# A decode step of sliding-window attention plus an MLP on one core: the order of V, w2 and P V, where 1/sum is applied, and which engine makes the tables

## The chip, the cores and the metric

The kernel runs on one core of a Trainium2 chip. The metric is device time in microseconds (us) of one execution. TensorE (PE) multiplies matrices, VectorE (DVE) and ScalarE (ACT) work elementwise, GpSimd (POOL) does here only memsets and small tables, and SyncE (SP) issues the transfers. Each engine runs its own program in order, and semaphores order the engines among each other. The transfers issued by SyncE go through one queue, over 16 DMA engines, in the order of issue.

## The reference

One token, x of 1024 elements, goes through a layer norm; the result feeds an attention with a cache and an MLP, and both are added to x's sum:

```python
def _A_ref(x, k_cache, v_cache, wq, wo):      # x: [1, 1, 1024]
    W = 4096                                  # the last 4096 of 65536 positions
    q = (x @ wq).reshape(1, 1, 32, 128).transpose(0, 2, 1, 3)
    k = jnp.repeat(k_cache[:, :, Sk - W:, :], 8, axis=1)     # 4 kv heads for 32 heads
    v = jnp.repeat(v_cache[:, :, Sk - W:, :], 8, axis=1)
    p = _softmax(jnp.einsum("bhqd,bhkd->bhqk", q, k) * 128 ** -0.5)
    o = jnp.einsum("bhqk,bhkd->bhqd", p, v)
    return o.transpose(0, 2, 1, 3).reshape(1, 1, 4096) @ wo

def _B_ref(x, w1, b1, w2, b2):
    h = _gelu(_layernorm(x) @ w1 + b1)        # 1024 -> 3584
    return h @ w2 + b2                        # 3584 -> 1024

xn = _layernorm(x)
return x + _A_ref(xn, ...) + _B_ref(xn, ...)
```

All inputs are bf16. Read are w1 and w2 (7.3 MB each), the windows of K and V (4.2 MB each), wq and wo (8.4 MB each): nearly 40 MB for one token.

## The kernel before

With one row of activations, every weight is read once and streams through TensorE as the moving operand, 512 columns at a time; the stationary operand is a column of 128 activations, padded to 32 columns. Matmuls of that shape use a quarter of the array, so several go side by side into different groups of 32 partitions.

**Transfers.** SyncE issues W1, K (two halves) and wq (two halves) at once. Then it waits for the product with W1 (`C["h"]`, L365) and issues w2, which takes W1's place in SBUF, and V in two halves (`load_cache`, L366 and L367). V's region is not free from the start: the row of b1 is laid in it (`B1R`, L138), and matmuls read it ahead of the product with W1. After the product with wq (`C["q"]`, L480), SyncE issues wo in six pieces of 16, 8, 4, 2, 1 and 1 rows of blocks (`WO_CHUNKS`), into wq's place.

**The order on TensorE.** Everything is written out by hand, and loops are rolled: `rolled` (L161) makes a loop whose body holds the matmuls of one step, with addresses in registers; a semaphore may be waited for in each round, against the register `trip`. In order: the norm's sums; b1 (L350); h = y W1 in 8 rounds (L362); transposes of h; q in 8 rounds, as the halves of wq come; transposes of q and its copies into `LB`; the scores, 32 matmuls (L470), with one maximum for each half; the maximum turned and spread (L492, L501) into `BIAS`. Then `steps("w2", ...)` (L506), 4 rounds of 14 matmuls into the accumulator `acc` (bank 7 of PSUM). ScalarE meanwhile takes the exponential in four quarters (L508), and VectorE transposes each quarter into `PT` (L512). TensorE then makes the sums of the rows with a matmul against `SAME` (L518), and runs P V (L529), 4 rounds of 8 matmuls, into bank 4.

**From P V to O.** VectorE takes the reciprocal of the sums (L533) and multiplies the masks `BLK` with it into `RG` (L535), four scalars for each partition. P V leaves four blocks of 128 columns, of which each partition needs one: ScalarE copies the first scaled by `RG[:, 0]` (L540), VectorE adds the three others scaled likewise (L543), into `OD`. Four matmuls against `E4` (L551) put `OD` in the layout that wo needs, and a copy (L555) writes it into `VEC` as `OT`.

**wo and the end.** `steps("wo", ...)` (L560) runs 3 rounds of 8 rows as the first two pieces land, four rows follow one by one, and the last four rows are cut into four quarters of 256 columns, which go side by side into another bank (L569). While these last rows come, ScalarE and VectorE copy the accumulated rows out into `PART` (L585); one add (L590) joins both, and a transfer of 2 KB writes the result.

**Tables.** VectorE makes, between the norm and the first transposes of K, the zeros of `LB`, `VEC` and `E4` and the tables `BLK`, `HD`, `REP4`, `SAME` and `E4` from an identity that GpSimd has filled (L296 to L315).

Of the kernel before, what the change touches and what calls it, by code (L numbers as in the profile page):

```python
# [10 lines left out]
D = 1024  # L11
# [40 lines left out]
def bass_parallel_sum__sliding_block_cached__mixer_channel_mlp__decode_kernel(  # L52
# [43 lines left out]
    E4 = sb("E4", [128, 4 * 129], f32)  # L96
    HD = sb("HD", [128, 2 * HQ], f32)
    REP4 = sb("REP4", [128, 4 * 128], bf16)
# [19 lines left out]
    U2 = sb("U2", [128, FC], f32)  # L118
    VEC = sb("VEC", [128, FC + 32 + PAD], bf16)
    GT = VEC[:, 0:FC]  # L120
    OT = VEC[:, FC:FC + 32]
    MXP = sb("MXP", [128, 3], f32)
# [5 lines left out]
    REC = sb("REC", [128, 1], f32)  # L128
    RG = sb("RG", [128, 4], f32)
    OD = sb("OD", [128, DH], f32)  # L130
# [29 lines left out]

    def rolled(label, n, streams, body, sem=None, ready=None):  # L161
        places = []
        for (view, step, weights), regs in zip(streams, (wregs, vregs)):
            span = bass.RuntimeValue.of_register_unchecked(zero, min_val=0, max_val=step * (n - 1))
            aps = view(span)
            low = pe.lower_ap(aps[0], for_matmul_weights=weights)
            pe.reg_add(regs[0], bass_rust.RegisterHandle(low.regref, pe.engine), 0)
            places.append([(mybir.RegisterAccessPattern(
                ap=low.ap, dtype=low.dtype, memsetref=low.memsetref, regref=reg.name,
                is_regloc_offset=low.is_regloc_offset, reg_ap_offset=reg.name, const_ap_offset=low.const_ap_offset,  # L170
                const_sub_tensor_id=low.const_sub_tensor_id, bass_ap=ap),
                reg, 2 * (ap.offset.min_val - aps[0].offset.min_val)) for ap, reg in zip(aps, regs)])
        pe.reg_mov(trip, 1)
        if ready is not None:
            pe.wait_ge(DVE.sem, ready)
        pe.br(f"L_{label}")
        nc.switch_bb(f"L_{label}", parent=None)
        if sem is not None:
            pe.wait_ge(sem, trip)
        for place in places:  # L180
            for _, reg, by in place[1:]:
                pe.reg_add(reg, place[0][1], by)
        last = body([p for p, _, _ in places[0]], [p for p, _, _ in places[1]])
        for place, (_, step, _) in zip(places, streams):
            pe.reg_add(place[0][1], place[0][1], 2 * step)
        pe.reg_add(trip, trip, 1)
        pe.br_lt(trip, n + 1, on_true=f"L_{label}", on_false=f"E_{label}")
        nc.switch_bb(f"E_{label}", parent=None)
        return last
# [41 lines left out]
    POOL.mark(pool.memset(OUTM[:, :], OUTSIDE))  # L231
    C["mask"] = fill(OUTM[:, :].rearrange("k (s g) -> k s g", g=2), [[0, 256], [1, 2]], 0, -1, value=0.0)


# [20 lines left out]
    for r in range(KC):  # L255
# [39 lines left out]
    C["zo"] = DVE.mark(dve.memset(PS[:, 4 * 512:5 * 512], 0.0))  # L295
    C["lb"] = DVE.mark(dve.memset(LB[:, :], 0.0))  # L296
    DVE.mark(dve.memset(VEC[:, :], 0.0))
    DVE.mark(dve.memset(E4[:, :], 0.0))
    dve.wait_ge(POOL.sem, C["identf"])
    DVE.mark(dve.tensor_reduce(out=BLK[:, :], in_=identf[:, :].rearrange("p (i q h) -> p q i h", i=NPAIR, q=4),  # L300
                               axis=AX.XY, op=ALU.add))
    DVE.mark(dve.tensor_reduce(out=HD[:, 0:HQ], in_=identf[:, :].rearrange("p (q h) -> p h q", q=4),
                               axis=AX.X, op=ALU.add))
    DVE.mark(dve.tensor_reduce(out=HD[:, HQ:2 * HQ].rearrange("p (i h) -> p i h", i=NPAIR),
                               in_=identf[:, :].rearrange("p (i q h) -> p i h q", i=NPAIR, q=4), axis=AX.X, op=ALU.add))
    C["rep4"] = DVE.mark(dve.tensor_copy(
        REP4[:, :].rearrange("p (e q d) -> p e q d", e=4, q=4),
        identf[:, :].rearrange("p (e d) -> p e d", e=4).unsqueeze(2).to_broadcast([128, 4, 4, 32])))
    dve.wait_ge(DVE.sem, DVE.cnt)
    C["same"] = DVE.mark(dve.tensor_copy(  # L310
        SAME[:, :].rearrange("p (i q h) -> p i q h", i=NPAIR, q=4),
        HD[:, 0:HQ].rearrange("p (i h) -> p i h", i=NPAIR).unsqueeze(2).to_broadcast([128, NPAIR, 4, 16])))
    C["consts"] = DVE.mark(dve.tensor_copy(
        E4[:, :].rearrange("p (q r) -> p q r", r=129)[:, :, 0:128:4],
        HD[:, HQ:2 * HQ].unsqueeze(1).to_broadcast([128, 4, HQ])))  # L315

# [33 lines left out]
    for t in range(7):  # L350
        last = tile(part(t, 0), oneb[64:65, :], b1v[:, :, :, 4 * t:4 * t + 4], (32, 32), (64, 32 * (t % 4)), t < 4, True)
    C["b1"] = PE.mark(last)
    pe.wait_ge(DVE.sem, C["y"])
    pe.wait_ge(POOL.sem, C["pads"])
# [11 lines left out]
    sp.dma_start(W2, w2_p).then_inc(s_w2, 16)  # L366
    load_cache(V, A_v_cache, s_v)  # L367
    for j, n in enumerate(WQ_CHUNKS):
# [70 lines left out]
    pe.wait_ge(DVE.sem, C["d_QT"])  # L439
    pe.wait_ge(DVE.sem, C["rep4"])  # L440
    for e in range(4):
# [3 lines left out]
    for eng, track, qs in ((dve, DVE, (0, 1)), (act, ACT, (2, 3))):  # L445
        eng.wait_ge(PE.sem, C["rep"])
        eng.wait_ge(DVE.sem, C["lb"])
        for q in qs:
            dst = LB8[32 * q:32 * q + 32, :, 32 * q:32 * q + 16]
            src = PS[32 * q:32 * q + 32, 6 * 512:6 * 512 + 128].rearrange("p (e h) -> p e h", e=8)  # L450
            C["lb", q] = track.mark(dve.tensor_copy(dst, src) if eng is dve  # L451
                                    else act.activation(out=dst, in_=src, func=ACTF.Copy))
# [51 lines left out]
    act.wait_ge(DVE.sem, C["bias"])  # L504
    pe.wait_ge(s_w2, 16)
    steps("w2", W2, 0, FC, 7)  # L506
    for n in range(4):
# [7 lines left out]
    C["tot"] = DVE.mark(dve.tensor_reduce(out=SUMP[:, :], in_=SUMS[:, :], axis=AX.X, op=ALU.add))  # L515
    pe.wait_ge(DVE.sem, C["tot"])
    pe.wait_ge(DVE.sem, C["same"])
    C["rows"] = PE.mark(pe.matmul(PS[:, 6 * 512 + 130:6 * 512 + 131], lhsT=SAME[:, :], rhs=SUMP[:, :]))  # L518
    pe.wait_ge(DVE.sem, C["zo"])
# [3 lines left out]
    def pv_rows(ws, vs):  # L523
# [6 lines left out]
        (lambda o: [V[:, bass.ds(o + i * 2 * W + j * 512, 512)] for j in range(4) for i in range(NPAIR)], 2048, False),  # L530
        (lambda o: [PT[:, bass.ds(o + i * 1024 + j * 64, 64)] for j in range(4) for i in range(NPAIR)], 256, True)), pv_rows)
    dve.wait_ge(PE.sem, C["rows"])
    DVE.mark(dve.reciprocal(out=REC[:, :], in_=PS[:, 6 * 512 + 130:6 * 512 + 131]))  # L533
    dve.wait_ge(DVE.sem, DVE.cnt)
    C["rg"] = DVE.mark(dve.tensor_scalar(out=RG[:, :], in0=BLK[:, :], scalar1=REC[:, 0:1], scalar2=None, op0=ALU.mult))  # L535
    dve.wait_ge(DVE.sem, DVE.cnt)
    dve.wait_ge(PE.sem, C["pv"])
    act.wait_ge(DVE.sem, C["rg"])
    act.wait_ge(PE.sem, C["pv"])
    C["a_od"] = ACT.mark(act.activation(out=OD[:, :], in_=PS[:, 4 * 512:4 * 512 + 128], func=ACTF.Copy, scale=RG[:, 0:1]))  # L540
    dve.wait_ge(ACT.sem, C["a_od"])
    for c in range(1, 4):
        C["d_od"] = DVE.mark(dve.scalar_tensor_tensor(  # L543
            out=OD[:, :], in0=PS[:, 4 * 512 + 128 * c:4 * 512 + 128 * c + 128], scalar=RG[:, c:c + 1], in1=OD[:, :],
            op0=ALU.mult, op1=ALU.add))
        if c < 3:
            dve.wait_ge(DVE.sem, DVE.cnt)
    pe.wait_ge(DVE.sem, C["consts"])
    pe.wait_ge(DVE.sem, C["d_od"])
# [4 lines left out]
    dve.wait_ge(PE.sem, C["o2"])  # L554
    C["OT"] = DVE.mark(dve.tensor_copy(OT, PS[:, 6 * 512 + 160:6 * 512 + 192]))  # L555
    looped = sum(WO_CHUNKS[:LOOPED])
    for j in range(LOOPED):
        sp.wait_ge(s_wo[j], 16)  # L558
        sp.nop(hint="wo").then_inc(s_go, WO_CHUNKS[j] // STEP)
    steps("wo", WA, FC, looped, STEP, s_go, C["OT"])  # L560
    quad = [PS[32 * a:32 * a + 32, 0:256] for a in range(4)]
    c0 = looped
    for j in range(LOOPED, len(WO_CHUNKS)):
        pe.wait_ge(s_wo[j], 16)
        for c in range(c0, c0 + WO_CHUNKS[j]):
            if j < HALVES:
                last = row(VEC[:, FC + c:FC + c + 32], WA[:, c * D:c * D + 512], WA[:, c * D + 512:(c + 1) * D])
            else:
                for a in range(4):  # L569
                    last = put(quad[a], VEC[:, FC + c:FC + c + 32], WA[:, c * D + a * 256:c * D + (a + 1) * 256], a,  # L570
                               start=(j == HALVES))
        c0 += WO_CHUNKS[j]
        if j == HALVES - 1:
            C["most"] = PE.mark(last)
# [49 lines left out]
```

## Time and profile before

| what | us |
|---|---|
| timed runs, median of 3 | 101.35 (99.96 to 101.4) |
| the profiled execution | 99.7 |
| its span, first to last instruction | 98.4 |
| busy: PE / DVE / ACT / POOL | 51.7 / 38.8 / 9.5 / 4.8 |
| bytes read from HBM | 39.86 MB, 405 GB/s over the span |
| h: product with W1 | 20.71 to 26.3 |
| q: last half of wq | 49.50 to 53.1 |
| scores | 56.66 to 66.3 |
| `OT` written (L555) | 84.03 to 84.22 |
| last wo rows | 95.84 to 96.2 |

The page of the profile gives shares by engine, forty slices of the span with the TensorE clock granted in each, the queues, and the chain of waits that ended last. A time such as "20.71" is counted from the span's start. A wait names the instruction or transfer that ended it. The granted clock is a share of full speed: at 0.50 a matmul takes twice as long as at 1.00. Idle time of an engine costs nothing unless the chain runs through it.

### The profile page before, as it was taken

What the parts mean: (1) busy time and instruction counts of PE and PEld (TensorE: products, weight loads), DVE (VectorE), ACT (ScalarE), POOL (GpSimd) and SP (SyncE); (2) the same over time, 40 slices, a digit from 0 to 9 for tenths busy, and PEclk for the clock granted to TensorE, in tenths of its full rate; (3) what the DMA queues carried; (4) which work ended last, traced back from release to release, by engine and by line L of the source; (5) the groups of instructions that cost most, each with busy time, mean ns of one, the idle gap of its engine ahead of it and who ended that gap; (6) DMA issues with size and microseconds to landing.
All of it is one profiled execution on the core that took longest, in us unless ns stands there. A gap on an engine that the chain in (4) does not pass through costs nothing.

```text
span 98.4 us, 964 instructions
## 1 busy us (share of the span) xinstructions
PE 51.7 (52%) x371; PEld 18.3 (19%) x292; DVE 38.8 (39%) x68; ACT 9.5 (10%) x22; POOL 4.8 (5%) x16
## 2 busy tenths in 40 slices
PE   0403300059620700760086499993899993189960
PEld 1302000013110000100021311211345543034420
DVE  0585880000899999993002300407560104000031
ACT  0502400000210000000002200000830001000030
POOL 6940000000000000000000000000000000000000
PEclk9999999999999555555555555899579999958999
DMA  9698889999999999999988899959999999999950
GB/s 374 280 469 373 374 373 396 429 426 426 453 533 426 426 426 426 426 426 426 586 373 373 373 419 632 419 230 426 426 426 446 426 426 453 413 426 413 400 226 7
DMA packets 2062, 39.88 MB, mean 405 GB/s; under 512 B 262, under 2 KB 266, under 8 KB 652
## 3 DMA queue, kind: packets, MB, share of 16 engines
q1 hardware_dynamic: 2024, 39.85, 94.8%
q8 instruction: 1, 0.02, 0.1%
q10 hardware_dynamic: 36, 0.01, 0.0%
q14 instruction: 1, 0.01, 0.0%
HBM read 39.86 MB, written 0.00 MB: 405 GB/s over the span
## 4 chain that ended last, share of the span: by engine, by line
DMA 88%; SPq 4%; PE 4%; issue 1%; DVE 0%; DVEq 0%
DMA WW<-in_A_wq_dram 47%; DMA WW<-in_A_wo_dram 41%; PE PS L332 4%; SPq L194 3%; SPq L202 1%; DVE ORow L590 0%; SPq L211 0%; DVEq L589 0%; SPq L369 0%
## 5 line engine op out<-in xcount | busy, mean ns | idle before, releaser
L324 DVE STREAM_TRANSPOSE KV<-KV 128x2048 bf16<-128x2048 bf16 x8 | 18.5, 2310 | 10.8 <-DMA KV<-in_A_k_cache_dram 10.6
L332 PE MATMUL PS<-WW,VEC 128*32 (+2 forms) x128 | 16.5, 421 | 3.8 <-SPq L558 2.6
L332 PE MATMUL PS<-WW,XNTb 128*32 x64 | 7.2, 630 | 11.8 <-SPq L369 11.8
L332 PE MATMUL PS<-WW,YTb 128*32 x56 | 5.6, 532 | 10.1 <-DMA WW<-in_B_w_dram 10.1
L332 PE MATMUL PS<-KV,LB 128*128 128x512 bf16 x31 | 9.6, 485 | 1.1 <-DVE LB L451 1.1
L332 PEld LDWEIGHTS PS<-WW,VEC 128*32 (+1 forms) x128 | 6.9, 108 | 12.9 <-issue 7.1
L479 DVE TENSOR_REDUCE MXP<-PS 128x1 f32<-128x1024 f32 x2 | 2.4, 1224 | 8.9 <-PE PS L332 8.9
L586 DVE COPY KV<-PS 32x256 f32<-32x256 f32 x2 | 0.8, 420 | 10.3 <-PE PS L332 10.2
L332 PEld LDWEIGHTS PS<-WW,XNTb 128*32 x32 | 1.3, 123 | 18.2 <-issue 18.2
L332 PEld LDWEIGHTS PS<-WW,YTb 128*32 x32 | 1.6, 116 | 14.3 <-issue 14.1
L332 PE MATMUL PS<-OUTM,PAR 2*128 2x512 bf16 x4 | 1.9, 614 | 4.2 <-DVE HT L396 4.2
L508 ACT ACTIVATE KV<-PS,BIAS 128x512 bf16<-128x512 f32 x4 | 2.7, 685 | 13.2 <-DVE BIAS L503 13.2
L428 DVE CAST Qs<-PS 128x512 bf16<-128x512 f32 x1 | 0.7, 691 | 8.1 <-PE PS L332 8.1
L332 PE MATMUL PS<-KV 128*64 x32 | 3.6, 380 | 0.0
L332 PEld LDWEIGHTS PS<-KV,LB 128*128 128x128 bf16 x16 | 1.9, 120 | 8.2 <-issue 7.4
L512 DVE STREAM_TRANSPOSE KV<-KV 128x512 bf16<-128x512 bf16 x4 | 2.7, 711 | 0.9 <-ACT KV L508 0.9
L282 PE MATMUL PS<-YT,onesf 128*128 128x16 f32 x2 | 0.6, 384 | 3.9 <-DVE YT L280 3.9
L543 DVE SCALAR_TENSOR_TENSOR OD<-PS,RG,OD 128x128 f32<-128x128 f32 x3 | 1.1, 351 | 3.8 <-ACT OD L540 3.7
L426 ACT ACTIVATE Qs<-PS 128x512 bf16<-128x512 f32 x1 | 0.6, 597 | 20.1 <-PE PS L332 20.1
L218 POOL TENSOR_SCALAR_AFFINE_SELECT OUTM<-OUTM 2x512 bf16<-2x512 bf16 x1 | 2.3, 2304 | 0.1
L372 ACT ACTIVATE Hs<-PS 128x512 bf16<-128x512 f32 x1 | 0.6, 598 | 15.4 <-PE PS L332 15.4
L551 PE MATMUL PS<-OD,E 128*128 128x32 f32 x8 | 1.1, 275 | 1.9 <-DVE OD L543 1.9
(96 smaller groups left out, 35.3 us busy)
## 6 DMA issues: line engine op xcount, KB each, us to landing
WW<-in_B_w_dram SPq DMA_DIRECT2D x2, 7168.0 KB, 29.8
WW<-in_A_wq_dram SPq DMA_DIRECT2D x2, 4096.0 KB, 41.4
KV<-in_A_k_cache_dram SPq DMA_DIRECT2D x2, 2048.0 KB, 25.8
KV<-in_A_v_cache_dram SPq DMA_DIRECT2D x2, 2048.0 KB, 46.9
WW<-in_A_wo_dram SPq DMA_DIRECT2D x1, 4096.0 KB, 32.9
WW<-in_A_wo_dram SPq DMA_DIRECT2D x1, 2048.0 KB, 37.4
WW<-in_A_wo_dram SPq DMA_DIRECT2D x1, 1024.0 KB, 39.3
WW<-in_A_wo_dram SPq DMA_DIRECT2D x1, 512.0 KB, 40.1
```

The source lines that it names most:

```text
L194: sp.dma_start(dst[:, c0 * width:(c0 + n) * width].rearrange("p (c n) -> p c n", c=n), src[:, c0:c0 + n, :],).then_inc(semaphores[j], 16)
L202: sp.dma_start(dst[:, 2 * i * W:2 * (i + 1) * W], cache[0, 2 * i:2 * i + 2, SK - W:SK, :].rearrange("g (m b) d -> m g (b d)", m=64),).then ...
L218: return POOL.mark(pool.affine_select(out=out, in_=out, pattern=pattern, compare_op=op, fill=value, base=base, channel_multiplier=step))
L324: C["kd"] = DVE.mark(dve.transpose(out=KD4[:, n], in_=KR[:, n * 2048:(n + 1) * 2048].rearrange("p (b e s) -> p b e s", b=16, e=4)))
L332: return pe.add_instruction(mybir.InstMatmult(name=nc.get_next_instruction_name(), engine=pe.engine, ins=[lowered(rhs, False), lowered(lhs ...
L428: C["d_qs"] = DVE.mark(dve.tensor_copy(Qs[:, 512:1024], PS[:, 7 * 512:8 * 512]))
L479: DVE.mark(dve.tensor_reduce(out=MXP[:, half:half + 1], in_=PS[:, half * 1024:(half + 1) * 1024], axis=AX.X, op=ALU.max))
L508: C["exp"] = ACT.mark(act.activation(out=Pb[:, n * 512:(n + 1) * 512], in_=PS[:, n * 512:(n + 1) * 512], func=ACTF.Exp, bias=BIAS[:, :], s ...
L512: C["tr", n] = DVE.mark(dve.transpose(out=PT.rearrange("p (i c h) -> p c i h", i=NPAIR, h=16)[:, 16 * n:16 * n + 16], in_=Pb[:, n * 512:(n ...
L543: C["d_od"] = DVE.mark(dve.scalar_tensor_tensor(out=OD[:, :], in0=PS[:, 4 * 512 + 128 * c:4 * 512 + 128 * c + 128], scalar=RG[:, c:c + 1], ...
L551: last = pe.matmul(PS[:, 6 * 512 + 160:6 * 512 + 192], lhsT=E4[:, dq * 128:(dq + 1) * 128], rhs=OD[:, dq * 32:(dq + 1) * 32], start=(dq == ...
L586: else dve.tensor_copy(dst, src))
```

## The change

V is issued ahead of w2, as soon as b1's matmuls have read V's region. P V is moved ahead of w2's loop, and each of its rounds waits for the transpose of its own quarter. The masks `BLK` are used as they are in `OD`; 1/sum is applied when `OT` is written, and the matmul of the sums stands behind P V, in another bank. w2's loop stands between O and wo. `OT` gets 32 zero columns ahead of it in `VEC`, so that the last block of w2's activations, whose operand is 32 columns wide, doesn't reach into it. GpSimd makes the zeros and the tables (except `BLK`): three memsets, the copy into `REP4`, and five adds for `HD`, `SAME` and `E4`; the memsets, reductions and copies on VectorE go. VectorE, ScalarE and TensorE wait for GpSimd's semaphore instead.

```diff
-    VEC = sb("VEC", [128, FC + 32 + PAD], bf16)
+    VEC = sb("VEC", [128, FC + PAD + 32 + PAD], bf16)
...
-    def rolled(label, n, streams, body, sem=None, ready=None):
+    def rolled(label, n, streams, body, sem=None, ready=None, first=0):
...
-        pe.reg_mov(trip, 1)
+        pe.reg_mov(trip, first + 1)
...
+    POOL.mark(pool.memset(VEC[:, :], 0.0))
+    C["lb"] = POOL.mark(pool.memset(LB[:, :], 0.0))
+    POOL.mark(pool.memset(E4[:, :], 0.0))
...
+    POOL.mark(pool.tensor_tensor(out=HD[:, 0:64], in0=identf[:, 0:64], in1=identf[:, 64:128], op=ALU.add))
...
+    for i in range(NPAIR):
+        C["consts"] = POOL.mark(pool.tensor_tensor(
+            out=E4[:, :].rearrange("p (q r) -> p q r", r=129)[:, :, 64 * i:64 * i + 64:4],
+            in0=HD4[:, i, 0, :].unsqueeze(1).to_broadcast([128, 4, 16]),
+            in1=HD4[:, i, 1, :].unsqueeze(1).to_broadcast([128, 4, 16]), op=ALU.add))
...
-    C["lb"] = DVE.mark(dve.memset(LB[:, :], 0.0))
-    DVE.mark(dve.memset(VEC[:, :], 0.0))
-    DVE.mark(dve.memset(E4[:, :], 0.0))
-    dve.wait_ge(POOL.sem, C["identf"])
+    dve.wait_ge(POOL.sem, C["lb"])
...
     C["b1"] = PE.mark(last)
+    sp.wait_ge(PE.sem, C["b1"])
+    load_cache(V, A_v_cache, s_v)
...
     sp.wait_ge(PE.sem, C["h"])
     sp.dma_start(W2, w2_p).then_inc(s_w2, 16)
-    load_cache(V, A_v_cache, s_v)
...
     act.wait_ge(DVE.sem, C["bias"])
-    pe.wait_ge(s_w2, 16)
-    steps("w2", W2, 0, FC, 7)
...
-    pe.wait_ge(DVE.sem, C["tot"])
-    C["rows"] = PE.mark(pe.matmul(PS[:, 6 * 512 + 130:6 * 512 + 131], lhsT=SAME[:, :], rhs=SUMP[:, :]))
...
...
-        (lambda o: [PT[:, bass.ds(o + i * 1024 + j * 64, 64)] for j in range(4) for i in range(NPAIR)], 256, True)), pv_rows)
-    DVE.mark(dve.reciprocal(out=REC[:, :], in_=PS[:, 6 * 512 + 130:6 * 512 + 131]))
-    C["rg"] = DVE.mark(dve.tensor_scalar(out=RG[:, :], in0=BLK[:, :], scalar1=REC[:, 0:1], scalar2=None, op0=ALU.mult))
-    act.wait_ge(DVE.sem, C["rg"])
+        (lambda o: [PT[:, bass.ds(o + i * 1024 + j * 64, 64)] for j in range(4) for i in range(NPAIR)], 256, True)),
+        pv_rows, DVE.sem, first=C["tr", 0] - 1)
+    pe.wait_ge(DVE.sem, C["tot"])
+    C["rows"] = PE.mark(pe.matmul(PS[:, 5 * 512:5 * 512 + 1], lhsT=SAME[:, :], rhs=SUMP[:, :]))
...
+    dve.wait_ge(PE.sem, C["rows"])
+    DVE.mark(dve.reciprocal(out=REC[:, :], in_=PS[:, 5 * 512:5 * 512 + 1]))
     pe.wait_ge(DVE.sem, C["d_od"])
...
-    C["OT"] = DVE.mark(dve.tensor_copy(OT, PS[:, 6 * 512 + 160:6 * 512 + 192]))
+    C["OT"] = DVE.mark(dve.tensor_scalar(
+        out=OT, in0=PS[:, 6 * 512 + 160:6 * 512 + 192], scalar1=REC[:, 0:1], scalar2=None, op0=ALU.mult))
...
-    steps("wo", WA, FC, looped, STEP, s_go, C["OT"])
+    pe.wait_ge(s_w2, 16)
+    steps("w2", W2, 0, FC, 7)
+    steps("wo", WA, FC + PAD, looped, STEP, s_go, C["OT"])
```

More of the change, by code (lines that the diff above doesn't have):

```diff
@@ L96, in bass_parallel_sum__sliding_block_cached__mixer_channel_mlp__decode_kernel @@
     E4 = sb("E4", [128, 4 * 129], f32)
-    HD = sb("HD", [128, 2 * HQ], f32)
+    HD = sb("HD", [128, 4 * HQ], f32)
     REP4 = sb("REP4", [128, 4 * 128], bf16)
@@ L118, in bass_parallel_sum__sliding_block_cached__mixer_channel_mlp__decode_kernel @@
     U2 = sb("U2", [128, FC], f32)
-    VEC = sb("VEC", [128, FC + 32 + PAD], bf16)
+    VEC = sb("VEC", [128, FC + PAD + 32 + PAD], bf16)
     GT = VEC[:, 0:FC]
-    OT = VEC[:, FC:FC + 32]
+    OT = VEC[:, FC + PAD:FC + PAD + 32]
     MXP = sb("MXP", [128, 3], f32)
@@ L128, in bass_parallel_sum__sliding_block_cached__mixer_channel_mlp__decode_kernel @@
     REC = sb("REC", [128, 1], f32)
-    RG = sb("RG", [128, 4], f32)
     OD = sb("OD", [128, DH], f32)
@@ L186, in rolled @@
         pe.reg_add(trip, trip, 1)
-        pe.br_lt(trip, n + 1, on_true=f"L_{label}", on_false=f"E_{label}")
+        pe.br_lt(trip, first + n + 1, on_true=f"L_{label}", on_false=f"E_{label}")
         nc.switch_bb(f"E_{label}", parent=None)
@@ L232, in bass_parallel_sum__sliding_block_cached__mixer_channel_mlp__decode_kernel @@
     C["mask"] = fill(OUTM[:, :].rearrange("k (s g) -> k s g", g=2), [[0, 256], [1, 2]], 0, -1, value=0.0)
+    POOL.mark(pool.memset(VEC[:, :], 0.0))
+    C["lb"] = POOL.mark(pool.memset(LB[:, :], 0.0))
+    POOL.mark(pool.memset(E4[:, :], 0.0))
+    POOL.mark(pool.tensor_copy(
+        REP4[:, :].rearrange("p (e q d) -> p e q d", e=4, q=4),
+        identf[:, :].rearrange("p (e d) -> p e d", e=4).unsqueeze(2).to_broadcast([128, 4, 4, 32])))
+    POOL.mark(pool.tensor_tensor(out=HD[:, 0:64], in0=identf[:, 0:64], in1=identf[:, 64:128], op=ALU.add))
+    pool.wait_ge(POOL.sem, POOL.cnt)
+    POOL.mark(pool.tensor_tensor(
+        out=SAME[:, :].rearrange("p (h b) -> p h b", b=4), in0=HD[:, 0:32].unsqueeze(2).to_broadcast([128, HQ, 4]),
+        in1=HD[:, 32:64].unsqueeze(2).to_broadcast([128, HQ, 4]), op=ALU.add))
+    parts = identf[:, :].rearrange("p (i q h) -> p i q h", i=NPAIR, q=4)
+    POOL.mark(pool.tensor_tensor(out=HD[:, 64:128].rearrange("p (i q h) -> p i q h", i=NPAIR, q=2),
+                                 in0=parts[:, :, 0:2, :], in1=parts[:, :, 2:4, :], op=ALU.add))
+    pool.wait_ge(POOL.sem, POOL.cnt)
+    HD4 = HD[:, 64:128].rearrange("p (i q h) -> p i q h", i=NPAIR, q=2)
+    for i in range(NPAIR):
[3 more added lines that the diff above has]
+            in1=HD4[:, i, 1, :].unsqueeze(1).to_broadcast([128, 4, 16]), op=ALU.add))
     def stats(src, ms, veps):
@@ L295, in bass_parallel_sum__sliding_block_cached__mixer_channel_mlp__decode_kernel @@
     C["zo"] = DVE.mark(dve.memset(PS[:, 4 * 512:5 * 512], 0.0))
-    C["lb"] = DVE.mark(dve.memset(LB[:, :], 0.0))
-    DVE.mark(dve.memset(VEC[:, :], 0.0))
-    DVE.mark(dve.memset(E4[:, :], 0.0))
-    dve.wait_ge(POOL.sem, C["identf"])
+    dve.wait_ge(POOL.sem, C["lb"])
     DVE.mark(dve.tensor_reduce(out=BLK[:, :], in_=identf[:, :].rearrange("p (i q h) -> p q i h", i=NPAIR, q=4),
                                axis=AX.XY, op=ALU.add))
[L302 to L315, printed above, removed]
     KD4 = KD.rearrange("p (n e b s) -> p n b e s", n=8, e=4, b=16)
@@ L439, in bass_parallel_sum__sliding_block_cached__mixer_channel_mlp__decode_kernel @@
     pe.wait_ge(DVE.sem, C["d_QT"])
-    pe.wait_ge(DVE.sem, C["rep4"])
+    pe.wait_ge(POOL.sem, C["consts"])
     for e in range(4):
@@ L446, in bass_parallel_sum__sliding_block_cached__mixer_channel_mlp__decode_kernel @@
         eng.wait_ge(PE.sem, C["rep"])
-        eng.wait_ge(DVE.sem, C["lb"])
+        eng.wait_ge(POOL.sem, C["lb"])
         for q in qs:
@@ L515, in bass_parallel_sum__sliding_block_cached__mixer_channel_mlp__decode_kernel @@
     C["tot"] = DVE.mark(dve.tensor_reduce(out=SUMP[:, :], in_=SUMS[:, :], axis=AX.X, op=ALU.add))
-    pe.wait_ge(DVE.sem, C["tot"])
-    pe.wait_ge(DVE.sem, C["same"])
-    C["rows"] = PE.mark(pe.matmul(PS[:, 6 * 512 + 130:6 * 512 + 131], lhsT=SAME[:, :], rhs=SUMP[:, :]))
     pe.wait_ge(DVE.sem, C["zo"])
@@ L530, in bass_parallel_sum__sliding_block_cached__mixer_channel_mlp__decode_kernel @@
         (lambda o: [V[:, bass.ds(o + i * 2 * W + j * 512, 512)] for j in range(4) for i in range(NPAIR)], 2048, False),
-        (lambda o: [PT[:, bass.ds(o + i * 1024 + j * 64, 64)] for j in range(4) for i in range(NPAIR)], 256, True)), pv_rows)
-    dve.wait_ge(PE.sem, C["rows"])
-    DVE.mark(dve.reciprocal(out=REC[:, :], in_=PS[:, 6 * 512 + 130:6 * 512 + 131]))
-    dve.wait_ge(DVE.sem, DVE.cnt)
-    C["rg"] = DVE.mark(dve.tensor_scalar(out=RG[:, :], in0=BLK[:, :], scalar1=REC[:, 0:1], scalar2=None, op0=ALU.mult))
-    dve.wait_ge(DVE.sem, DVE.cnt)
+        (lambda o: [PT[:, bass.ds(o + i * 1024 + j * 64, 64)] for j in range(4) for i in range(NPAIR)], 256, True)),
+        pv_rows, DVE.sem, first=C["tr", 0] - 1)
+    pe.wait_ge(DVE.sem, C["tot"])
+    C["rows"] = PE.mark(pe.matmul(PS[:, 5 * 512:5 * 512 + 1], lhsT=SAME[:, :], rhs=SUMP[:, :]))
     dve.wait_ge(PE.sem, C["pv"])
-    act.wait_ge(DVE.sem, C["rg"])
     act.wait_ge(PE.sem, C["pv"])
-    C["a_od"] = ACT.mark(act.activation(out=OD[:, :], in_=PS[:, 4 * 512:4 * 512 + 128], func=ACTF.Copy, scale=RG[:, 0:1]))
+    C["a_od"] = ACT.mark(act.activation(out=OD[:, :], in_=PS[:, 4 * 512:4 * 512 + 128], func=ACTF.Copy, scale=BLK[:, 0:1]))
     dve.wait_ge(ACT.sem, C["a_od"])
@@ L543, in bass_parallel_sum__sliding_block_cached__mixer_channel_mlp__decode_kernel @@
         C["d_od"] = DVE.mark(dve.scalar_tensor_tensor(
-            out=OD[:, :], in0=PS[:, 4 * 512 + 128 * c:4 * 512 + 128 * c + 128], scalar=RG[:, c:c + 1], in1=OD[:, :],
+            out=OD[:, :], in0=PS[:, 4 * 512 + 128 * c:4 * 512 + 128 * c + 128], scalar=BLK[:, c:c + 1], in1=OD[:, :],
             op0=ALU.mult, op1=ALU.add))
@@ L547, in bass_parallel_sum__sliding_block_cached__mixer_channel_mlp__decode_kernel @@
             dve.wait_ge(DVE.sem, DVE.cnt)
-    pe.wait_ge(DVE.sem, C["consts"])
+    dve.wait_ge(PE.sem, C["rows"])
+    DVE.mark(dve.reciprocal(out=REC[:, :], in_=PS[:, 5 * 512:5 * 512 + 1]))
     pe.wait_ge(DVE.sem, C["d_od"])
@@ L554, in bass_parallel_sum__sliding_block_cached__mixer_channel_mlp__decode_kernel @@
     dve.wait_ge(PE.sem, C["o2"])
-    C["OT"] = DVE.mark(dve.tensor_copy(OT, PS[:, 6 * 512 + 160:6 * 512 + 192]))
+    dve.wait_ge(DVE.sem, DVE.cnt)
+    C["OT"] = DVE.mark(dve.tensor_scalar(
+        out=OT, in0=PS[:, 6 * 512 + 160:6 * 512 + 192], scalar1=REC[:, 0:1], scalar2=None, op0=ALU.mult))
     looped = sum(WO_CHUNKS[:LOOPED])
@@ L566, in bass_parallel_sum__sliding_block_cached__mixer_channel_mlp__decode_kernel @@
             if j < HALVES:
-                last = row(VEC[:, FC + c:FC + c + 32], WA[:, c * D:c * D + 512], WA[:, c * D + 512:(c + 1) * D])
+                last = row(VEC[:, FC + PAD + c:FC + PAD + c + 32], WA[:, c * D:c * D + 512], WA[:, c * D + 512:(c + 1) * D])
             else:
                 for a in range(4):
-                    last = put(quad[a], VEC[:, FC + c:FC + c + 32], WA[:, c * D + a * 256:c * D + (a + 1) * 256], a,
+                    last = put(quad[a], VEC[:, FC + PAD + c:FC + PAD + c + 32], WA[:, c * D + a * 256:c * D + (a + 1) * 256], a,
                                start=(j == HALVES))
```

## The prediction

> **What bounds the kernel now.** I read the page first: busy shares, slices, the queue table, the chain. The profiled execution took 99.7 us, its span is 98.4, so 1.3 us lie around the span. The three timed runs gave 99.96, 101.35 and 101.4 (median 101.35): two near the profiled time, two 1.5 us above it. About 2% either way is what a measurement of this kernel can tell from no change.
>
> ```profile
> PEclk9999999999999555555555555899579999958999
> DMA  9698889999999999999988899959999999999950
> q1 hardware_dynamic: 2024, 39.85, 94.8%
> DMA 88%; SPq 4%; PE 4%; issue 1%; DVE 0%; DVEq 0%
> ```
>
> No engine is busy for more than 52% of the span; the transfer queue is, for 94.8% (0.948 x 98.4 = 93.3 us), and 88% of the chain is transfers. The chain of waits in order of time shows where the rest lies:
>
> ```profile
> 3.29 45.92 DMA WW<-in_A_wq_dram
> ...
> 49.50 3.62 PE PS L332 x32
> ...
> 55.42 40.38 DMA WW<-in_A_wo_dram
> ...
> 95.84 0.32 PE PS L332 x4
> ...
> 96.29 0.42 DVE ORow L590
> ```
>
> The 40.38 us of wo are mostly queueing: wo is issued at 53.1 to 55.9, behind w2 (7.34 MB) and V (4.19 MB). The PE step at 49.50 stands in the chain only because it releases that issue; the queue stayed full meanwhile, for the DMA share in the one-microsecond windows from 49 to 55 averages about 1. From its first packet near 2.0 us to 95.8 is 93.8 us, and 93.3 of them are busy: half a microsecond of gaps. Behind the last wo rows come only four matmuls, one add of 0.42 and the output transfer.
>
> Last, the timeline of the stages that move, for the room TensorE has:
>
> ```profile
> 69.36 0.69 ACT L508 ACTIVATE KV<-PS,BIAS 128x512 bf16<-128x512 f32 x1 [13.22 <-DVE BIAS L503]
> ...
> 69.48 7.70 PE L332 MATMUL PS<-WW,VEC 128*32 x56 [0.41 <-issue]
> ...
> 77.41 3.64 PE L332 MATMUL PS<-KV 128*64 x32
> ...
> 82.94 1.05 PE L551 MATMUL PS<-OD,E 128*128 128x32 f32 x8 [1.88 <-DVE OD L543]
> ...
> 86.62 7.78 PE L332 MATMUL PS<-WW,VEC 128*32 x56 [2.63 <-SPq L558]
> ```
>
> w2's loop runs from 69.5, P V from 77.4, O is in VEC at 84.2, and then TensorE waits 2.6 us for wo. So O has 2.4 us of room already, and making O earlier is worth nothing by itself.
>
> **Part one: V ahead of w2.** Bytes and transfers are the same. V's two issues (0.55 and 0.61 us) now stand behind a wait for the b1 matmuls, which end at 9.60 + 1.03 = 10.6. Behind that wait on SyncE only w2's issue is queued, and it waits for h until 26.36 anyway. The queue holds W1, K and both halves of wq until 49.2, so V joins 38 us and w2 some 23 us before the queue reaches them: no gap. At the windows' 426 GB/s V lands at 49.2 + 4.19/0.426 = 59.0 and w2 17.2 us later, at 76.3. Before, w2 landed at 66.7 (issue 26.4, and 40.3 to landing, from the two B_w loads' median 29.8 and W1's 19.3) and V at 76.4 (27.3 + 49.1). wo starts near 76.4 either way and ends at 95.8. Cost 0; bounds -0.5 (every gap gone) to +0.5 (a second set of gaps).
>
> **Part two: tables on GpSimd.** Off VectorE go memsets, reductions and copies from 11.78 to 14.38: nothing waits there until K lands at 25.0, worth 0. Onto GpSimd come three memsets, a copy and five adds. By the 512-wide memset's 0.52 us, LB (1152 wide) is 1.2, E4 0.5, VEC 0.1, the copy at least 0.5 and the adds 0.2 to 0.3 each: about 4 us after 5.98, ending near 10; by the OUTM select (2.30 for 512 elements) it would be four times that, 22. VectorE's new wait for LB is then over at 7.3 to 12, and behind it are the BLK reduction and K's first transpose at 25.0; the tables themselves are used at 55.2 and later. One row warns: the normalisation's scaling at L241 took 1.85 us beside that select, and 0.17 when it ran alone. The new GpSimd work runs beside the rest of that chain, whose tensor-scalar steps (y among them, at 9.71) may be held 1 to 2 us each. y is needed when W1 lands at 20.7, 10.7 us later. Cost 0; if that cover were gone, 2 to 6 us.
>
> **Part three: P V by quarters.** The exponentials and transposes don't move: BIAS at 69.26, transposes ending at about 70.9, 71.6, 72.2 and 72.9. P V takes 3.64 us at the full granted clock, 0.91 a quarter, so at best it ends at 72.9 + 0.9 = 73.8. But w2's loop no longer warms TensorE ahead of it. The windows show what a start after a pause costs:
>
> ```profile
> 71.00:72.00 1.00, 1.00 (x7) 0.37 (x5) 1.00 (x2) 1.00 (x4) 0.00 (x0) 0.50 1.03 442
> 72.00:73.00 1.00, 1.00 (x10) 0.55 (x8) 0.92 (x3) 0.14 (x2) 0.00 (x0) 0.75 1.07 459
> ...
> 88.00:89.00 1.00, 1.00 (x8) 0.34 (x6) 0.00 (x0) 0.00 (x0) 0.00 (x0) 0.50 1.07 459
> 89.00:90.00 1.00, 1.00 (x8) 0.36 (x6) 0.00 (x0) 0.00 (x0) 0.00 (x0) 0.72 0.85 360
> ```
>
> Third from the right in these windows stands the granted clock: a mean of 0.75 in one microsecond is a rise from 0.50 to 1.00 at 72.5, and 0.72 one at 89.6, 3.0 us after each loop began; for the scores it took 5.6 us (56.7 to 62.3). P V starts at 70.9 at 0.50, 1.82 us a quarter. With 3 us at half clock it ends at 70.9 + 3.64 + 1.5 = 76.0, with 5.6 at 77.3. I take 77.0, as the gated first quarters look more like the slow start, and go on from there. The Trainium skill, "TensorE: Matmul & The Clock Gate", Part 1, speaks against this part: the clock doubles only after a busy window of about 3.4 us, and the windows run free of the kernel. By that rule a start can stay at half clock for up to two windows, 6.8 us, and P V would end as late as 70.9 + 3.64 + 3.4 = 77.9. The trace agrees that the length varies (3.0, 3.0 and 5.6 us); the sum stays as it is.
>
> **Part four: 1/sum in the last copy.** The removed RG step (0.23) and the reciprocal (0.17) were done at 77.9, ahead of P V's end: worth 0 on the path. The matmul of the row sums (0.38) moves behind P V, beside the 1.5 us of OD's steps on ScalarE and VectorE; the reciprocal hides under the E4 matmuls (1.05). The last copy becomes a scaling: 0.19 to 0.29. From P V's end to OT were 84.22 - 81.05 = 3.2 us; now 3.3. OT at 80.3 instead of 84.2, and TensorE free at 80.0.
>
> **Part five: w2's loop after O.** Queued behind its wait on TensorE is wo alone. w2 has landed (76.4), so the loop starts at 80.0. 56 matmuls in pairs, 28 x 0.213 at full clock = 6.0, the row of before 7.7: it ends at 86.0 to 87.7, against wo's first rows at 86.6. wo's 28 rows of whole width then need 6.0 at full clock, but their last rows land at about 93.3, as before. The copies of PART may start as late as 95.2 before the last add (96.29) waits for them, so w2 may end as late as 89.2: 1.5 to 3.2 us of room, where the wo loop of before had 0.7 (its rows ended at 94.4). If w2 ends at 88 or earlier, wo goes straight on without the half clock that it had from 86.6 to 89.6.
>
> **Sum.** 0 + 0 + 0 + 0 + 0 on the profiled execution: span 98.4, 99.7 us.
>
> **Rivals.** *Late TensorE cured* (faster). The two runs at 101.4 may be ones in which wo's loop of before stayed at half clock. Never rising, 28 rows at 0.427 make 12.0 us, to 98.6, which puts the end 3.4 later; rising after 5.6 instead of 3.0 us costs 1.3, of which 0.7 is room, so 0.6. A mean of such starts can give the 1.6 between 99.7 and 101.35. With w2 running into wo it is gone: 99.7, 1.6% below the median; over 2% (under 99.3) only if a few tenths of gaps go as well. For it: 0.7 us of room is little, and the start-up length varies in the rows. Against: the four times fall in two tight pairs (99.7 and 99.96, 101.35 and 101.4), where start-ups of varying length would spread them, so something that the trace doesn't show may set them apart.
>
> *TensorE becomes the bound* (slower). All of w2 now stands after O. If start-ups are long, w2 takes 12.0 at half clock, ends at 92.0, and 28 rows at full clock bring 98.0, which is 2.8 past the 95.2 that is covered: 102.5. It decides from a w2 end later than 89.2; for over 2% above the median (103.4) TensorE must be 3.7 late, 13.8 us of half clock after 80. The longest stretch under steady work was 5.6. For it: two long loops end to end with no slack between. Against: P V keeps TensorE busy until 77, and after the similar gap at 81.05 to 82.94 the clock stayed at 1.00.
>
> *It doesn't do what it says.* If P V's quarters wait on something other than the transposes, or start cold, O is no earlier than 82: w2 ends at 88 to 90, and the time is 99.7 to 100.5, no change.
>
> **How the numbers follow.** Transfers decide, nothing changes: 0.55, with runs between 99.7 and 101.4; late TensorE cured: 0.33, 99.3 to 99.9, and I give 0.2 of it to over 2%, since part of the runs must be compared with 101.4; TensorE the bound: 0.12, 101 to 104, 0.08 of it over 2%. The third rival is inside the first's time. So faster 0.20, same 0.72, slower 0.08. The likeliest case leaves the runs as they are: between 99.7 and 101.4 I take the middle, 100.5. The range goes from the cured case with its gaps gone (99.2) to the median and the half microsecond of new gaps (101.9).
>
> **What would show it.** Right: wo's last transfer still ends near 95.8 with the queue at 95% and a chain of DMA; V landed by 59 and w2 at 76; P V from 70.9 at 0.50; OT near 80; w2's loop ending before 88 and wo at full clock from 86.6. Wrong: a hole in the DMA row between 49 and 77, y later than 20, or a chain whose end is w2 and wo on TensorE without waits for transfers.

## The result and the profile after

| | before | changed |
|---|---|---|
| median of 4 runs each, us | 100.66 (99.8 to 101.4) | 100.38 (100.3 to 100.53) |
| ratio, changed to before | | 1.0052, 95% interval 1.0027 to 1.0076 |
| profiled execution / its span, us | 99.7 / 98.4 | 100.3 / 99.1 |
| last landing of wo, us | 95.80 | 96.41 |

The ratio leaves out runs more than 1.5% above the fastest of their kernel; without the two at 101.35 and 101.4, before stands at 99.8 and 99.96, and no run of the changed kernel is as fast. So the change costs half a per cent against the usual run of before, and yet has the lower median, because none of its four runs is above 101, as two of before are. Both halves need a cause.

The page after, the lines that answer to those of before:

```profile
PEclk9999999999997555555555555998557999999999
DMA  9898889999999999999999998899988999799940
q1 hardware_dynamic: 2024, 39.85, 94.6%
DMA 88%; SPq 4%; PE 4%; issue 1%; DVE 0%; DVEq 0%
```

The queue was busy for 93.3 us before and is now for 0.946 x 99.1 = 93.7, with the same packets and bytes. The chain of waits in order of time:

```profile
3.25 46.24 DMA WW<-in_A_wq_dram
...
49.78 3.62 PE PS L337 x32
...
55.69 40.72 DMA WW<-in_A_wo_dram
...
96.45 0.32 PE PS L337 x4
...
96.90 0.42 DVE ORow L593
```

It is the same chain of transfers, 0.3 us later at wq's end and 0.6 at wo's; no wait was added to it. One pair of profiles can't say where along the transfers the loss arises: wq's end alone lies anywhere between 49.2 and 49.65 in the profiles kept of kernels whose packets keep the pace of before. The timeline of the stages that moved:

```profile
71.39 5.68 PE L337 MATMUL PS<-KV 128*64 x32 [2.20 <-DVE KV L516]
...
78.77 1.08 PE L550 MATMUL PS<-OD,E 128*128 128x32 f32 x8 [1.38 <-DVE OD L541]
...
79.78 6.22 PE L337 MATMUL PS<-WW,VEC 128*32 x56
...
87.00 3.63 PE L337 MATMUL PS<-WW,VEC 128*32 x32 [1.00 <-SPq L559]
```

P V starts behind the first transpose, w2's loop follows O, and wo waits for its landing. The windows answer to those of before (third from the right the granted clock):

```profile
74.00:75.00 1.00, 1.00 (x8) 0.50 (x6) 0.00 (x0) 0.00 (x0) 0.00 (x0) 0.50 0.00 0
75.00:76.00 1.00, 1.00 (x10) 0.41 (x6) 0.00 (x0) 0.00 (x0) 0.00 (x0) 0.72 1.22 524
...
87.00:88.00 1.00, 1.00 (x10) 0.53 (x12) 0.00 (x0) 0.00 (x0) 0.00 (x0) 1.00 1.04 442
```

P V starts at half clock, as forecast, and wo now runs at 1.00 from its first row.

### The profile page after: what moved, and what is told of

It is laid out like the page before. It is cut to its first block, busy times and chain, and to the rows that moved or that the text cites. A ratio compares the mean times of both kernels' runs of the same rounds, so it can differ in the third digit from the quotient of the medians.

```text
span 99.1 us, 962 instructions
## 1 busy us (share of the span) xinstructions
PE 51.1 (52%) x372; PEld 17.9 (18%) x292; DVE 37.2 (38%) x59; ACT 9.5 (10%) x22; POOL 8.6 (9%) x25
## 4 chain that ended last, share of the span: by engine, by line
DMA 88%; SPq 4%; PE 4%; issue 1%; DVE 0%; DVEq 0%
DMA WW<-in_A_wq_dram 47%; DMA WW<-in_A_wo_dram 41%; PE PS L337 4%; SPq L193 3%; SPq L201 1%; DVE ORow L593 0%; SPq L210 0%; DVEq L592 0%; SPq L375 0%
## 5 line engine op out<-in xcount | busy, mean ns | idle before, releaser
L337 PE MATMUL PS<-WW,VEC 128*32 (+2 forms) x128 | 13.8, 367 | 3.2 <-SPq L560 1.3
L337 PEld LDWEIGHTS PS<-WW,VEC 128*32 (+1 forms) x128 | 5.7, 97 | 11.1 <-issue 3.2
L337 PE MATMUL PS<-KV 128*64 x32 | 5.7, 533 | 2.2 <-DVE KV L516 2.2
L485 DVE TENSOR_REDUCE MXP<-PS 128x1 f32<-128x1024 f32 x2 | 2.4, 1224 | 8.6 <-PE PS L337 8.6
L337 PEld LDWEIGHTS PS<-KV 128*64 x32 | 2.4, 152 | 5.1 <-issue 4.7
L541 DVE SCALAR_TENSOR_TENSOR OD<-PS,BLK,OD 128x128 f32<-128x128 f32 x3 | 1.0, 350 | 4.7 <-ACT OD L538 4.6
L588 ACT ACTIVATE KV<-PS 32x256 f32<-32x256 f32 x2 | 0.7, 373 | 17.5 <-PE PS L337 17.5
```

Source lines behind the costliest of these rows:

```text
L337: return pe.add_instruction(mybir.InstMatmult(name=nc.get_next_instruction_name(), engine=pe.engine, ins=[lowered(rhs, False), lowered(lhs ...
L485: DVE.mark(dve.tensor_reduce(out=MXP[:, half:half + 1], in_=PS[:, half * 1024:(half + 1) * 1024], axis=AX.X, op=ALU.max))
L541: C["d_od"] = DVE.mark(dve.scalar_tensor_tensor(out=OD[:, :], in0=PS[:, 4 * 512 + 128 * c:4 * 512 + 128 * c + 128], scalar=BLK[:, c:c + 1] ...
L588: C["part", a // 2] = track.mark(act.activation(out=dst, in_=src, func=ACTF.Copy) if eng is act else dve.tensor_copy(dst, src))
```

## The experiments

The packet records of the traces were the first lead: in the profile of before every 32 KB packet took 1213 ns, in that of the changed kernel 1213 to 1224 (and one 1875). Two theories followed. "Pace": executions differ so by themselves. "Order" or "tables": a part of the change slows the transfers.

**The two kernels again.** No edit.

> The kernel before, unchanged, to see how much two executions of one program differ. The profile of before had 93.5 us of packets on each DMA engine (the packet records summed, over 16), all 32 KB packets at 1213 ns; the changed kernel had 93.8 us, at 1213 to 1224. If that pace belongs to the execution and not to the program (theory 'pace'), the records of this run lie between or beyond the two, ratio 1.000, and its times fall again in two groups near 99.9 and 101.4. If the pace belongs to the program (theories 'order' and 'tables'), every 32 KB packet is at 1213 again and the last wo rows land at 95.8. If the 101.4 runs of before come from a late TensorE (theory 'late TensorE'), a profile of such a run has wo's matmuls running past the last landing.

> The changed kernel, unchanged. Theory 'pace': the ratio to before goes to 1.000 within its interval, and the packets may be at 1213 ns. Theories 'order' and 'tables': 1.005 again, the last wo rows at 96.4 in the span again (95.8 before).

Before against itself: 1.000 (0.998 to 1.0021), packets at 1213 again. The changed kernel: 1.0086 (1.0053 to 1.0118), packets at 1213 to 1224 again, last wo rows at 96.6. The pace belongs to the program; "pace" fell.

**V ahead of w2, alone.**

```diff
     C["b1"] = PE.mark(last)
+    sp.wait_ge(PE.sem, C["b1"])
+    load_cache(V, A_v_cache, s_v)
...
     sp.dma_start(W2, w2_p).then_inc(s_w2, 16)
-    load_cache(V, A_v_cache, s_v)
```

> The kernel before with V issued ahead of w2 behind b1's wait, all else as before. Theory 'order': 100.3, ratio 1.005, landings of wo 0.3 to 0.6 late from the 49th us on. Theories 'tables' and 'pace': 99.9, ratio 1.000. The prediction's own: 0.

105.25 us at the median of eight runs, ratio 1.0375 (1.0343 to 1.0407): none of the expectations. The timeline of TensorE shows what they left out:

```profile
77.50 7.65 PE L332 MATMUL PS<-WW,VEC 128*32 x56 [9.82 <-DMA WW<-in_B_w_dram]
...
85.39 3.64 PE L332 MATMUL PS<-KV 128*64 x32
...
93.00 8.35 PE L332 MATMUL PS<-WW,VEC 128*32 x72 [1.04 <-DVE VEC L556]
```

w2's loop still stands ahead of P V, and now waits until 77.5 for a w2 that lands last; O comes at 92, and wo's rows run past their landing. The order of transfers and of loops can only be moved together. But the packets are at exactly 1213 ns: the order doesn't slow them.

**Tables on GpSimd, alone.** The table lines of the diff, and the waits that go with them.

> The kernel before with the tables made on GpSimd, all else as before. Theory 'tables': W1's product starts 0.1 later, wq lands 0.25 later, 100.1 to 100.4, ratio 1.002 to 1.005. Theories 'order' and 'pace': 99.9, ratio 1.000. In each, y is ready near 11.1, 1 us later than before, behind 9 us of cover.

99.94 us, 0.9986 (0.9955 to 1.0017), packets at 1213: "tables" fell too. What was left was no step of the program but where its buffers lie. In the built programs each buffer takes a multiple of 32 bytes of each partition. HD grew by 256, VEC from 192 to 256, RG's 32 went: +288, so KV moved from byte 36352 (142 x 256) to 36640 (143 x 256 + 32), and WW behind it likewise. The tables-only kernel moved both by 256.

**The address, taken away and put in.** The edits of four kernels:

```diff
-    SUMS = sb("SUMS", [128, 4], f32)
-    SUMP = sb("SUMP", [128, 1], f32)
+    SUMX = sb("SUMX", [128, 5], f32)
+    SUMS = SUMX[:, 0:4]
+    SUMP = SUMX[:, 4:5]
```

in the changed kernel, and in the others `GAP = sb("GAP", [128, n], bf16)` ahead of KV: n = 16 in before, 16 in the changed kernel, 64 in before.

> The changed kernel with the row sums in the same small tensor as their total, which saves 32 bytes of SBUF for each partition: KV and WW then begin at a multiple of 256 bytes, as they do in the kernel before and in the two runs with packets at exactly 1213 ns; in the changed kernel they begin 32 bytes past one. Theory 'address' (the pace of the packets comes from where their destination begins): 32 KB packets at 1213 ns, packets summed 93.5 us, last wo rows near 95.9, 99.9 us, ratio 1.000. Theory 'order' (w2 straight ahead of wo, or V ahead of w2, costs the half per cent): 1213 to 1224 again, 100.4 to 100.6, ratio 1.005 to 1.009.

> The kernel before with 32 unused bytes ahead of KV, nothing else. Theory 'address': 32 KB packets at 1213 to 1224 ns, packets summed 93.8 us, 100.3 to 100.6 us, ratio 1.005. Theory 'order': 1213, ratio 1.000.

> The changed kernel with 32 unused bytes ahead of KV, so that KV and WW begin at a multiple of 64 bytes, 64 past a multiple of 256. If 64 bytes are enough: 1213 ns and ratio 1.000, as the run at a multiple of 256. If the price is that of not beginning at a multiple of 256: 1215 to 1224, ratio 1.005. Theory 'order': 1.005 to 1.009 whatever the address.

> The kernel before with 128 unused bytes ahead of KV, so that KV and WW begin 128 bytes past a multiple of 256. If a destination has to begin at a multiple of 256: 32 KB packets at 1213 to 1224 ns, ratio 1.005 to 1.009 as with 32 and 64 bytes. If 128 is enough: all at 1213, ratio 1.000.

| kernel | KV and WW past a multiple of 256 | 32 KB packet, ns (mean) | span, median us | ratio to before |
|---|---|---|---|---|
| before (again) | 0 | 1213.0 | 98.7 | 1.000 (0.998 to 1.0021) |
| tables only | 0 | 1213.0 | 98.7 | 0.9986 (0.9955 to 1.0017) |
| changed, 32 bytes saved | 0 | 1214.4 | 98.55 | 0.9999 (0.9967 to 1.003) |
| changed (again) | 32 | 1217.4 | 99.3 | 1.0086 (1.0053 to 1.0118) |
| before, 32 added | 32 | 1216.6 | 99.3 | 1.0089 (1.0054 to 1.0124) |
| changed, 32 added | 64 | 1216.1 | 99.1 | 1.0094 (1.0054 to 1.0133) |
| before, 128 added | 128 | 1214.7 | 99.2 | 1.0054 (1.0026 to 1.0082) |

Thirty-two unused bytes make the kernel before as slow as the changed one, and 32 bytes saved make the changed one as fast as before. (The 1214.4 of the third row holds one packet of 1.7 us, and 1217.4 and 1216.1 one of 1.9 us each; without it they are 1213.0, 1215.7 and 1214.4. The 90th percentile is 1213 in the first three rows, against 1220 to 1224 below.) The ratios differ more than the spans: "before, 32 added" holds one late run (span 100.2), and the two sets of the changed kernel hold runs with about 2 us around the span, of which more below.

The ends of two of the chains, the changed kernel with 32 bytes saved and then the kernel before with 32 added:

```profile
55.32 40.62 DMA WW<-in_A_wo_dram
...
96.42 0.42 DVE ORow L594
```

```profile
55.63 40.77 DMA WW<-in_A_wo_dram
...
96.88 0.42 DVE ORow L591
```

wo lands at 95.94 and at 96.40. In all seven profiles at a multiple of 256 whose chain ends in that landing it lies between 95.80 and 96.14, in the five past one between 96.32 and 96.60. The Trainium skill, "DMA: Bandwidth & Descriptors", section "How a descriptor splits into AXI transactions", says that a read which starts off a multiple of 256 bytes begins at the boundary below, and that the bytes ahead of the start are fetched unused and still cost transfer beats. No run here moved the side that is read. The runs show a price for the place in SBUF that is written, at each of 32, 64 and 128 bytes past; per packet it is less at 64 and 128 than at 32, and how the address makes a packet longer is not shown.

**The runs above 101.** In 114 runs of before, the span goes with the mean granted clock:

```
mean clock       runs   span us: lowest, median, highest
0.785 to 0.800    26    98.7   98.9   99.2
0.800 to 0.811    24    98.4   98.7   98.9
0.812 to 0.813    15    99.8  100.0  100.2
above 0.815       49    98.4   98.6   99.0
```

So the late group has one mean clock. (It isn't equally frequent everywhere: 6 of 35, 6 of 27, 3 of 29 and none of 23 in the four sets of runs.) Two theories: "wo's start" (wo's loop stays at half clock for long), and "starved P V" (P V waits for V, runs at half clock, O is late). Ten matmuls were put into before ahead of wo, and in another kernel ahead of P V:

```diff
+    for _ in range(10):
+        pe.matmul(PS[:, 5 * 512:6 * 512], lhsT=identb[:, :], rhs=W2[:, 0:512])
```

> The kernel before with ten matmuls of 512 columns between O and wo (into a bank that nobody reads, 2.1 us at full clock), nothing else, so that TensorE's pause ahead of wo shrinks from 2.6 us to under 1. Theory 'late TensorE' for the runs of before at 101.3 to 101.5 (span 100.0, mean clock 0.812; 5 of 23): none of them among 11 or 12 runs, spans 98.5 to 98.9 only, and the runs at a mean clock of 0.79 (span 98.9 to 99.2) gone too; wo's matmuls from 86.6 at a clock of 1.00. Rival (something outside TensorE): the group at 100.0 comes again, one run in five or six. On the median ratio both give 0.998 to 1.000.

1.0019 (0.9979 to 1.0059), but six of 12 spans at 99.9 to 101.0, more than without: the expectation missed. Its profile (span 100.0), the timeline of TensorE:

```profile
77.59 6.32 PE L332 MATMUL PS<-KV 128*64 x32 [3.26 <-DMA KV<-in_A_v_cache_dram]
...
87.29 3.39 PE L555 MATMUL PS<-WW,identb 128*128 128x512 bf16 x9 [0.22 <-issue]
90.61 6.66 PE L332 MATMUL PS<-WW,VEC 128*32 x72
```

P V waited 3.26 us for V, ran at half clock (6.32 instead of 3.64), O came at 87.3, and the added matmuls then delayed wo further.

> The kernel before with ten matmuls of 512 columns (2.1 us at full clock, into a bank that nobody reads) between w2's loop and P V. Six of 27 runs of before have a span of 99.8 to 100.1 at a mean clock of 0.812. Theory 'starved P V': in these the scores and w2's loop fell into full clock early, w2 ended near 74, TensorE waited over 3 us for V (lands 76.4 to 77.5), P V ran at half clock and O came after wo's first rows. Then the added matmuls fill that pause, P V runs at full clock, and none of 12 runs has a span over 99.4. Rival 'wo's start' (the runs come from wo's own cold start, whatever P V did): two or three of 12 at 99.8 to 100.1 again. Median ratio by both 1.000 to 1.003.

1.0003 (0.9979 to 1.0028), spans 98.5 to 99.4 in 12 runs, where 3 of the 29 of before beside it went to 100.1 and more. No late group, as "starved P V" expects; but at 15 in 114, twelve runs without one happen one time in five.

> The kernel before with five matmuls of 512 columns in the three short pauses between q and the scores (two, one and two, into a bank that nobody reads), so that TensorE is busy from 49.5 to 56.3 and the scores start at full clock in every run. Theory 'starved P V': the scores end near 63.3 instead of 66.3, w2's loop starts when w2 lands (66.7) and ends at 73 to 76, TensorE waits for V until 76.4 to 77.5, P V runs at half clock (5 to 6.3 us), O comes at 85 to 87 and wo's rows late: with TensorE faster in its middle the kernel is slower, most runs at a span of 99.2 to 100.2, median 100.6 to 101.4, ratio 1.006 to 1.014. Rival 'wo's start' and the prediction's own reading (TensorE's middle is off the path): the distribution of before, three runs of four at 98.4 to 98.8, ratio 1.000.

1.0003 (0.9977 to 1.0028), spans 98.5 to 99.2: a miss for "starved P V" in that form, which had expected most runs to be late. (None of the 23 runs of before beside it was late either.) In its profile TensorE paused only 1.0 us ahead of P V, which then ran at full clock (3.64 us). The chain of that profile (span 99.2) ends otherwise:

```profile
86.92 9.64 PE PS L332 x62
...
97.09 0.42 DVE ORow L596
```

wo's loop itself. Four further executions of before, no edit, none of them in the late group, three in the group at 0.793:

> One look at the kernel before, unchanged, in the hope of a profile in the late group (span 99.8 to 100.2 at a mean clock of 0.812, about one run in six). In such a profile 'starved P V' expects P V at half clock, ending after 83, and O after 86.6; 'wo's start' expects P V ending near 81 and O near 84 as in the profile of before, and wo's rows at half clock for over 5 us from 86.6. Both expect a chain that ends in wo's matmuls and not in the last landing.

> As for the look before it: the kernel before once more, a second execution, with the same two readings of a late profile if it is one (P V ending after 83, or wo's rows at half clock for over 5 us).

> As for the look before it: the kernel before once more, a third execution, with the same two readings of a late profile if it is one (P V ending after 83, or wo's rows at half clock for over 5 us).

> As for the look before it: the kernel before once more, a fourth execution, with the same two readings of a late profile if it is one (P V ending after 83, or wo's rows at half clock for over 5 us).

Spans 99.0, 99.1, 98.8 and 98.7. In the first three the chain ends in wo's matmuls; the first one's chain, and its windows:

```profile
86.87 8.95 PE PS L332 x56
...
96.80 0.42 DVE ORow L590
```

```profile
85.00:86.00 1.00, 0.36 (x4) 0.24 (x3) 0.19 (x1) 0.00 (x0) 0.00 (x0) 0.78 0.96 410
...
91.00:92.00 1.00, 1.00 (x8) 0.35 (x6) 0.00 (x0) 0.00 (x0) 0.00 (x0) 0.50 1.02 434
92.00:93.00 1.00, 1.00 (x10) 0.43 (x8) 0.00 (x0) 0.00 (x0) 0.00 (x0) 0.81 0.96 373
```

The clock stays at 0.50 until 92.4, 5.5 us after wo's start, where the profile of before had 3.0: the last add at 96.80 instead of 96.29. "wo's start" is shown for these runs of the group at 0.793, whose usual span is 98.9. Which step makes the group at 100.0 stays open: no profile of the unchanged kernel fell into it.

**Parts of the change, with the address mended.** The transfers in the old order:

> The changed kernel with KV and WW at a multiple of 256 again, but w2 issued ahead of V as before. P V then waits for V until 76.4 or later and starts at half clock: it ends at 81.6 to 83.5, O 3.2 later, w2's loop of 6.2 to 9.1 ends at 91 to 96, and wo's 28 rows need 6.0 more, against the 95.2 that is covered: 1.8 to 6.6 late, 101.5 to 106 us, ratio 1.02 to 1.06. If the order of V and w2 did not matter to the rest of the change, 99.8 as with V first.

104.22 us (101.92 to 104.63 in 4 runs). The timeline of TensorE:

```profile
77.02 5.96 PE L338 MATMUL PS<-KV 128*64 x32 [8.14 <-DMA KV<-in_A_v_cache_dram]
...
86.12 13.89 PE L338 MATMUL PS<-WW,VEC 128*32 x128
```

As expected: w2 and wo end to end behind a late O.

P V behind all four transposes, by `pv_rows, ready=C["tr", 3]`:

> The changed kernel with KV and WW at a multiple of 256 again, and P V started only when all four quarters are transposed, instead of quarter by quarter. P V and O come 1 to 1.5 us later; w2's loop ends at 85 to 90, before 89.2 in nearly all runs. By the prediction's reading the gate is worth nothing: 99.8 us, ratio 1.000, spans 98.4 to 98.8. If the early start of P V is what keeps the late group away, spans of 99.4 and more come back in one run of five.

1.0032 (0.9997 to 1.0066), five of 12 spans at 99.0 to 99.6, where the gated kernel had none above 98.7: the gate seems to be worth something in runs with a low clock (the five are at 0.776 to 0.811), though the ratio doesn't settle it, and the two kernels ran on different chips.

The five matmuls of e14 in the changed kernel:

> The same five matmuls in the changed kernel with KV and WW at a multiple of 256. V has landed by 59, so P V starts two or three microseconds earlier, w2's loop still waits for w2 until 76.4, and nothing is starved. Theory 'starved P V': all runs at 98.4 to 98.8, median 99.8, ratio 1.000 or below. Rival: no different from the kernel before with the same five matmuls.

1.0037 (1.0008 to 1.0066), spans 98.6 to 99.1, no late run; but before had none in 23 beside it, so that tells little. The ratio is above the spans because four runs had 1.9 to 2.4 us around the span instead of 1.3, for which no trace has a cause. Runs with over 1.8 us around the span are more frequent with both new orders, 13 of 54, than in before, 5 of 114; whether the change causes them stays open.

In the five kernels with both new orders (54 runs) no span is over 99.6, although 18 of the runs have the shifted address; of before it is 15 in 114, and of before with a shifted address 2 in 18. That the orders do this isn't shown: the tables-only kernel, in the old order, had all 12 spans at 98.7, at clocks from 0.792 to 0.857. At the 6 late runs in 35 of before beside it, twelve without one happen one time in ten.

## Why the prediction failed

**The bound** was right: the transfers set the end, in both profiles.

**Parts one to five** were right to within half a microsecond: y at 11.1 behind 9.7 us of cover; P V ending at 77.07 (forecast 77.0), `OT` at 80.14 (80.3), w2's loop from 79.78 to 86.0 (80.0 to 86.0 or 87.7), wo at full clock. That P V's end came out so close is luck: it began 0.5 late, at 71.39 (the first transpose ends at 70.94, as forecast; the sum had left out the loop's own start, in the row of w2's loop before 0.41 us of "issue"), and it was at half clock for 4.2 us where 77.0 assumes 4.9. That the new order opens no gap in the queue is confirmed by wo's last landing in the three kernels with both new orders and the address of before: 95.94, 96.14 and 96.02, where before and the tables-only kernel have 95.80 to 96.02.

**The sum** is the step that failed. It had a term for each instruction and each wait that moved, and none for the buffers whose sizes change. The diff's lines on HD, VEC and RG were read as free; they put KV and WW 32 bytes past a multiple of 256, which costs some 3 ns in each of the 112 packets of 2 KB and more of a DMA engine: the records add up to 0.3 us more for each. The rest of the later landing lies in part behind the last packet, whose end is followed by the landing after 0.30 to 0.36 us in the seven profiles at a multiple of 256 and after 0.46 to 0.48 in the five past one. The term is 0.5 us, 0.5% (means of these profiles' last landings: 95.98 and 96.45); with the address mended the ratio is 0.9999. "Bounds -0.5 to +0.5" for the queue's gaps hid it without naming it.

**The forecast's level.** 100.5 was chosen as the middle of two pairs of runs and stood below the median of before, which made it a forecast of a gain. With 114 runs the usual span is 98.7, and the 101.35 that I measured against has the time of a group of 15.

**Late TensorE cured** was right in its size for one start (wo's loop at half clock for 5.5 us moves the last add by 0.5; forecast 0.6), but that explains spans near 98.9 and not the runs at 101.4, for which the prediction used it. The late group is absent in 54 runs of the new orders; that their order is the cause, and what makes the group, stay open. **TensorE the bound** did not decide, but its price is real where one of the orders is missing: 104 to 105 us. **The gate** was counted as nothing; e13 speaks mildly against that, and doesn't settle it.

## What to carry to other kernels

When transfers set a kernel's time, a diff's buffer sizes are part of its cost: compare the start addresses of the transfers' destinations before and after, and keep them at multiples of 256 bytes. Here a packet time that was constant in one profile and scattered in another came from the address, and not from the program's order. The changed kernel with 32 bytes saved is as fast as before in its usual runs and has no late ones in 12 runs: 99.81 us at the median against 100.0 for before in the same comparison, ratio 0.9999 (0.9967 to 1.003), no span over 98.7.

## What was not expected of the hardware

The price of a destination that doesn't begin at a multiple of 256 bytes: in the changed kernel 2 to 5 ns in packets of all sizes (means: 2 KB 84.0 to 86.4, 8 KB 309.1 to 314.3, 32 KB 1213.0 to 1217.6; median of 56 KB: 2116 to 2120). And how far one program's executions differ along with the clock: before has spans from 98.4 to 100.2, and the late ones all have a mean granted clock of 0.812 or 0.813.
